# Sparse attention with a gated projection: the products with V in 128x64 instead of 128x32 tiles of TensorE

## The chip, the core and the metric

The kernel runs on one core of a Trainium2 chip. The metric is the device time of one execution in microseconds; lower is better. TensorE works on an array of 128 rows by 128 columns. A matmul whose stationary operand has 32 columns takes a 128x32 part of it (a column tile), one with 64 columns a 128x64 part. In the profile a shape such as 128*32 is rows times columns of the stationary operand, PE are the matmuls and PEld the weight loads that go before them.

## The reference

Eight batches of eight heads, 576 positions, 64 values a head, fp32. Heads 0 to 3 are local (a query sees itself and the 31 positions before it), heads 4 to 7 are strided (a query sees the earlier positions with the same remainder by 32). Then comes a gated projection.

```python
scores = scale * np.matmul(q, k.transpose(0, 1, 3, 2))
mask_local = (rel >= 0) & (rel < 32)
mask_strided = (rel >= 0) & (pos[None, :] % 32 == pos[:, None] % 32)
scores = np.where(masks, scores, -1e9)          # local for h < 4, strided for h >= 4
attn = softmax(scores)                          # exp(s - max) / (sum + 1e-9)
x = np.matmul(attn, v)                          # (B, H, S, 64) -> (B, S, 512)
gate = sigmoid(sum(conv_w[k] * xp[:, k:k + S, :] for k in range(5)))
out = (gate * (x @ w_val)) @ w_out
```

## The kernel before

Everything is planned first and issued later: each step (a matmul group, one vector instruction, one load) gets a number, and the string `SEQUENCE` near the end of the file holds the numbers of all steps in the order of issue, with `f0xN` for N filler matmuls at the start. What one engine executes is its own steps in that order; semaphores are placed from the data and the buffers. TensorE's steps are of these kinds:

- QK, local (`attend_local`, line 301, group `L b.u`): three steps a batch, 12 fp32 matmuls each into `s_ps`, stationary 32 queries (128x32), moving 128 columns.
- QK, strided (`attend_strided`, line 374, group `S b.u`): two steps a batch, 32 fp32 matmuls each into `s_ps`, stationary 128x32, moving 36 columns.
- transposes of the local weights into `t_ps`, 128x128, three or four a step.
- products with V, local: one step for each `L b.u`, 16 fp32 matmuls into `x_ps` (lines 358 to 362). The stationary operand is 32 columns of `vLs`, half a head, the moving one 96 columns of the block-diagonal weights `BDL`. The index `n` counts the four quarters of the 128 output rows, and `n // 2` is the head.
- products with V, strided: two steps for each `S b.u`, 16 matmuls each into `x_ps` (lines 409 to 413), stationary 32 columns of `vSs`, moving 72 columns of `BDS`.
- the value and output projections and, for two chunks of the first batch, the convolution, 128x128 in fp32r into `m_ps`.

There are 24 local and 32 strided steps of products with V in the eight batches. In the order of issue, TensorE goes from a QK step directly to a product with V 18 times (8 of them from local QK, 10 from strided QK), and from a product with V directly to a QK step 19 times (13 to local QK, 6 to strided QK). The other neighbours of these steps are transposes, projections or further products with V. ScalarE copies `x_ps` out, and softmax is shared by VectorE, ScalarE and GpSimd.

`x_ps` has two buffers, `s_ps` two, `t_ps` one, `m_ps` three. All steps are recorded by helpers, so the profile shows one line (L53) for nearly all of them; they are told apart by tile names.

Of the kernel before, what the change touches and what calls it, by code (L numbers as in the profile page):

```python
# [57 lines left out]
def tile_sparse_attention_moe(  # L58
# [34 lines left out]
    def dve(group, fn, **kw):  # L93
        plan.add("dve", group, [(fn, kw)])

    def act(group, fn, **kw):
        plan.add("act", group, [(fn, kw)])

    def gps(group, fn, **kw):
        plan.add("pool", group, [(fn, kw)])  # L100

    def pe(group, calls):
        plan.add("pe", group, calls)

    def mm(out, lhsT, rhs, first=True, last=True):
        return (T.matmul, dict(out=out, lhsT=lhsT, rhs=rhs, start=first, stop=last))
# [17 lines left out]
    vLs = pool.tile([P, 6, 256], F32, name="vLs")  # L124
    vSs = pool.tile([P, 8, 256], F32, name="vSs")
# [175 lines left out]
    def attend_local(b):  # L301
        xs = xss[b % 2]


        for u in range(3):
            group = f"L{b}.{u}"
            sp = s_ps.next()[:, :384]
            sv = sp.rearrange("r (k h w) -> r k h w", h=2, w=64)
            calls = []
            for k, j in enumerate((0, 2, 1)):  # L310
                for a in range(2):
                    for p in range(2):
                        c = 3 * (2 * u + a) + j
                        r0 = 32 * (2 * a + p)
                        calls.append(mm(sv[r0:r0 + 32, k, :, :], qLs[:, p, 32 * c:32 * c + 32],
                                        KBL[:, :, p, 32 * c:32 * c + 64]))
            wide = [P, 3, 2, 64]
            mask, mask_b = (m[:, None, None, :].to_broadcast(wide) for m in (maskL, maskLB))
            if u == 0:
                mask, mask_b = (m[:, :, None, :].to_broadcast(wide) for m in (maskF, maskFB))  # L320
            sm = SML.next()
            recip = softmax(group, sp, calls, mask, mask_b, sm.rearrange("p h k w -> p (h k) w"),
                            sm[..., 0:64].rearrange("p h k w -> p k h w"), "r (k h w) -> r k h w",
                            (b, "L", u) in ONPE).rearrange("p (h k) -> p h k", k=3)
            pw = PB.next()
            packed = pw.rearrange("p h w -> p (h w)")[:, :384]
            ends, middle = pw[:, :, 0:128], pw[:, :, 160:224]
            if b in PACKED:
                ends = packed[:, :256].rearrange("p (h w) -> p h w", h=2)
                middle = packed[:, 256:].rearrange("p (h w) -> p h w", h=2)  # L330
            gps(group, G.tensor_tensor, out=ends.rearrange("p h (k w) -> p h k w", w=64),
                in0=sm[:, :, 0:2, 0:64], in1=recip[:, :, 0:2, None].to_broadcast([P, 2, 2, 64]), op=ALU.mult)
            gps(group, G.tensor_tensor, out=middle, in0=sm[:, :, 2, 0:64],
                in1=recip[:, :, 2:3].to_broadcast([P, 2, 64]), op=ALU.mult)
            bd = BDL.next()
            if b in PACKED:
                tp = t_ps.next()[:, :384].rearrange("r (z g i) -> r z g i", z=3, i=32)
                pe(group, [
                    (T.transpose, dict(out=tp[:, z, :, :].rearrange("r g i -> r (g i)"), in_=packed[:, 128 * z:128 * z + 128],
                                       identity=ident[:, :]))  # L340
                    for z in range(3)])
                act(group, A.copy, out=bd[0:64, :, :, 0, :], in_=tp[0:64, 0:2])
                act(group, A.copy, out=bd[64:128, :, :, 2, :], in_=tp[64:128, 0:2])
                for h in range(2):
                    for i in range(2):
                        act(group, A.copy, out=bd[32 + 32 * i:64 + 32 * i, h, :, 1, :],
                            in_=tp[64 * h + 32 * i:64 * h + 32 * i + 32, 2])
            else:
                tp = t_ps.next().rearrange("r (h z g i) -> r h z g i", h=2, z=2, i=32)
                pe(group, [  # L350
                    (T.transpose, dict(out=tp[:, h, z, :, :].rearrange("r g i -> r (g i)"),
                                       in_=pw[:, h, 128 * z:128 * z + 128], identity=ident[:, :]))
                    for h in range(2) for z in range(2)])
                act(group, A.copy, out=bd[0:64, :, :, 0, :], in_=tp[0:64, :, 0])
                act(group, A.copy, out=bd[64:128, :, :, 2, :], in_=tp[64:128, :, 0])
                act(group, A.copy, out=bd[:, :, :, 1, :], in_=tp[:, :, 1])
            xp = x_ps.next()[:, :384].rearrange("r (p s) -> r p s", p=2)
            pe(group, [
                mm(xp[32 * n:32 * n + 32, p, 96 * a:96 * a + 96],
                   vLs[:, 2 * u + a, 128 * p + 32 * n:128 * p + 32 * n + 32],  # L360
                   bd[:, n // 2, 2 * a + p, :, :].rearrange("r j i -> r (j i)"))
                for a in range(2) for p in range(2) for n in range(4)])
            part = slice(192 * u, 192 * u + 192)
            if b in DIRECT:
                hi, lo = xhi[b % 2][:, 0:2, part], xlo[b % 2][:, 0:2, part]
                act(group, A.copy, out=hi, in_=xp)
                dve(group, V.tensor_tensor, out=lo, in0=xp, in1=hi.bitcast(F32), op=ALU.subtract)
                continue
            act(group, A.copy, out=xs[:, 0:2, PADK:][:, :, part], in_=xp)
        if b not in DIRECT:  # L370
            split_x(b, 0)
            split_x(b, 1)

    def attend_strided(b):
        xs = xss[b % 2]

        n = 16
        for u in range(2):
            group = f"S{b}.{u}"
            sp = s_ps.next()[:, :n * NT]  # L380
            sv = sp.rearrange("r (n t) -> r n t", t=NT)
            calls = []
            for p in range(2):
                for cc in range(4):
                    for g in range(4):
                        r0 = NT * (4 * (4 * u + cc) + g)
                        at = 8 * p + 2 * cc
                        calls.append(mm(sv[32 * g:32 * g + 32, at:at + 2, :],
                                        qSs[:, p * S + r0:p * S + r0 + 32],
                                        KBS[:, :, p, r0:r0 + NT]))  # L390
            pp = PS.next()
            sm = SMS.next()
            wide = [P, n, NT]
            recip = softmax(group, sp, calls, maskS[:, None, :].to_broadcast(wide),
                            maskSB[:, None, :].to_broadcast(wide), sm[:, :, :], sm[:, :, 0:NT],
                            "r (n w) -> r n w", (b, "S", u) in ONPE)

            for rows, keys in ((slice(0, 32, 2), slice(0, 16)), (slice(1, 32, 16), slice(16, NT))):
                gps(group, G.tensor_tensor, out=pp[:, :, rows], in0=sm[:, :, keys],
                    in1=recip[:, :, None].to_broadcast([P, n, keys.stop - keys.start]), op=ALU.mult)  # L400
            pt = PT.next()
            dve(group, V.transpose, out=pt.rearrange("r n t -> r (n t)"), in_=pp.rearrange("r n t -> r (n t)"))
            bd = BDS.next()
            for g in range(4):
                rows = slice(32 * g, 32 * g + 32)
                act(group, A.copy, out=bd[rows, :, g, :], in_=pt[rows, :, 0:NT])
            for p in range(2):
                xp = x_ps.next()[:, :288].rearrange("r (c q) -> r c q", c=4)
                pe(group, [
                    mm(xp[32 * n:32 * n + 32, cc, :],  # L410
                       vSs[:, 4 * u + cc, 128 * p + 32 * n:128 * p + 32 * n + 32],
                       bd[:, 8 * p + 2 * cc + n // 2, :, :])
                    for cc in range(4) for n in range(4)])
                act(group, A.copy,
                    out=xs[:, 2 + p, PADK:].rearrange("r (t c) -> r c t", c=STRIDE)[:, 16 * u:16 * u + 16, :],
                    in_=xp.rearrange("r c (g t) -> r (c g) t", t=NT))
                if u == 1:
                    split_x(b, 2 + p)
# [209 lines left out]
```

## Time and profile before

| what | value |
|---|---|
| median of 3 runs | 311.24 us (309.99 to 311.71) |
| profiled execution, first to last instruction | 308.1 us |
| TensorE busy | 297.6 us (97%) |
| VectorE, ScalarE, GpSimd busy | 75%, 74%, 63% |

The page gives the profiled execution's span, from its first to its last instruction; what lies around it is in the times of the runs alone. A row of the timeline merges instructions of one kind that follow each other: start, length from the first start to the last end, engine, operation, tiles, shapes, count. The start of the last instruction of such a row is start + length - duration of one. An fp32 matmul of the source has two matmul records and two weight loads in the trace. A matmul's end is modelled by the profiler, so the argument goes by starts.

### The profile page before, as it was taken

The page shows a single profiled execution, that of the slowest core. Times are in us where ns is not written, and L with a number is a line of the kernel's source. Part 1 is how long each engine was busy: PE and PEld are TensorE (multiplying, and loading weights), DVE is VectorE, ACT ScalarE, POOL GpSimd, SP SyncE. Part 2 cuts the span into 40 slices and gives each one's busy share as a digit, 9 for nine tenths or more (in the row PEclk, how much of TensorE's full clock was granted, in tenths as well). Part 3 has the DMA queues.
Part 4 walks back from the last instruction along what each step waited for, and adds up shares of the span by engine and source line. Part 5 has one row for each costly group of instructions (what it writes and reads, how often), then busy time and mean ns, then how long its engine had stood idle before and what let it go on. Part 6 is the DMA issues. An engine that isn't in the chain of part 4 may idle for free.

```text
span 308.1 us, 11209 instructions
## 1 busy us (share of the span) xinstructions
PE 297.6 (97%) x4770; PEld 261.4 (85%) x4773; DVE 231.1 (75%) x407; ACT 229.0 (74%) x501; POOL 193.5 (63%) x236
## 2 busy tenths in 40 slices
PE   8697999999999999999999999999999999999995
PEld 3376899988899789998899888998899789989983
DVE  4799499899998859858898788798956786695200
ACT  6667977998689769979989787967987848635221
POOL 8566899968695776558748695666446412562410
PEclk9979999999999999999999999999999999999999
DMA  7999597437655485534635336400133020011003
GB/s 229 351 285 281 191 278 234 139 102 233 207 150 194 145 251 193 158 79 155 190 116 161 96 145 209 141 6 0 70 104 129 36 105 34 3 68 70 0 34 136
DMA packets 20321, 43.99 MB, mean 143 GB/s; under 512 B 3056, under 2 KB 8944, under 8 KB 19696
## 3 DMA queue, kind: packets, MB, share of 16 engines
q1 hardware_dynamic: 20272, 43.28, 43.8%
q8 instruction: 37, 0.61, 0.8%
q14 instruction: 12, 0.10, 0.1%
HBM read 33.84 MB, written 9.44 MB: 140 GB/s over the span
## 4 chain that ended last, share of the span: by engine, by line
PE 89%; DMA 5%; DVE 2%; ACT 1%; POOL 1%; issue 1%; SPq 0%; DVEq 0%; POOLq 0%
PE m_ps L53 66%; PE x_ps L53 11%; PE s_ps L53 8%; PE t_ps L53 4%; DMA xs<-in_w_val_dram 2%; DMA KBL<-in_kL_dram 2%; DMA KBS<-in_kS_dram 1%; DVE ST L53 1%; DVE KBL L173 1%; PE m_ps L162 1%; POOL SML L53 0%; DVE SML L53 0%; POOL PB L53 0%; DVE gate L53 0%; ACT wv L53 0%
## 5 line engine op out<-in xcount | busy, mean ns | idle before, releaser
L53 DVE SCALAR_TENSOR_TENSOR gate<-xs,cw,gate 128x576 f32<-128x576 f32 x120 | 111.6, 948 | 4.8 <-ACT gate L53 4.0
L53 PE MATMUL m_ps<-xhi,wv 128*128 128x288 f32 x512 | 103.7, 297 | 0.0
L53 POOL TENSOR_TENSOR glo<-GV,ghi 128x288 fp32r<-128x288 f32 x64 | 56.0, 883 | 56.1 <-ACT ghi L53 55.7
L53 PE MATMUL m_ps<-wo,ghi 128*128 128x512 f32 x288 | 90.2, 394 | 0.0
L53 PEld LDWEIGHTS m_ps<-xhi,wv 128*128 128x128 f32 x512 | 82.1, 188 | 0.8
L53 PE MATMUL m_ps<-xlo,wv 128*128 128x288 f32 x256 | 75.6, 295 | 0.0
L53 PEld LDWEIGHTS m_ps<-wo,ghi 128*128 128x128 f32 x288 | 52.9, 188 | 11.1 <-issue 0.2
L53 PE MATMUL m_ps<-wo,glo 128*128 128x512 f32 x144 | 56.2, 390 | 0.0
L53 DVE SCALAR_TENSOR_TENSOR GV<-gate,m_ps 128x288 f32<-128x288 f32 x64 | 28.2, 445 | 33.8 <-POOL glo L53 14.2
L53 PEld LDWEIGHTS m_ps<-xlo,wv 128*128 128x128 f32 x256 | 48.1, 188 | 0.0
L53 POOL TENSOR_TENSOR PB<-SML,ST 128x128 f32<-128x128 f32 (+1 forms) x48 | 33.7, 715 | 17.6 <-DVE ST L53 11.6
L53 ACT CAST ghi<-GV 128x288 fp32r<-128x288 f32 x64 | 27.4, 431 | 19.8 <-DVE GV L53 19.2
L53 ACT COPY xs<-x_ps 128x288 f32<-128x288 f32 (+1 forms) x53 | 32.0, 611 | 9.5 <-PE x_ps L53 9.1
L53 ACT COPY BDL<-t_ps 64x256 f32<-64x256 f32 (+2 forms) x108 | 34.3, 319 | 6.2 <-PE t_ps L53 4.5
L53 ACT ACTIVATE osb<-m_ps 128x512 f32<-128x512 f32 x36 | 21.5, 601 | 21.2 <-PE m_ps L53 18.0
L53 PEld LDWEIGHTS m_ps<-wo,glo 128*128 128x128 f32 x144 | 27.0, 188 | 5.9
L53 ACT COPY BDS<-PT 32x288 f32<-32x288 f32 x64 | 27.7, 433 | 2.3 <-PE x_ps L53 1.1
L53 POOL TENSOR_TENSOR xlo<-xs,xhi 128x576 fp32r<-128x576 f32 x16 | 26.5, 1666 | 4.2 <-ACT xhi L53 4.2
L53 POOL TENSOR_TENSOR PS<-SMS,ST 128x256 f32<-128x256 f32 (+1 forms) x32 | 21.0, 669 | 11.7 <-DVE ST L53 11.6
L53 POOL TENSOR_TENSOR SML<-SML,ST 128x384 f32<-128x384 f32 x21 | 23.6, 1129 | 6.0 <-DVE ST L53 6.0
L53 DVE TENSOR_REDUCE ST<-SML 128x6 f32<-128x390 f32 (+1 forms) x45 | 24.2, 543 | 3.0 <-ACT SML L53 2.9
L53 ACT ACTIVATE gate<-xs,cw 128x576 f32<-128x576 f32 x30 | 23.2, 775 | 2.1 <-DVE GV L53 1.9
(91 smaller groups left out, 405.6 us busy)
## 6 DMA issues: line engine op xcount, KB each, us to landing
out_dram<-osb SPq DMA_DIRECT2D x36, 256.0 KB, 2.3
vLs<-in_vL_dram SPq DMA_DIRECT2D x8, 640.0 KB, 6.4
qLs<-in_qL_dram SPq DMA_DIRECT2D x16, 288.0 KB, 4.2
KBL<-in_kL_dram SPq DMA_DIRECT2D x16, 288.0 KB, 4.6
KBS<-in_kS_dram SPq DMA_DIRECT2D x16, 288.0 KB, 5.0
qSs<-in_qS_dram SPq DMA_DIRECT2D x16, 288.0 KB, 3.6
vSs<-in_vS_dram SPq DMA_DIRECT2D x32, 128.0 KB, 5.1
raw<-in_w_val_dram SPq DMA_DIRECT2D x2, 512.0 KB, 6.4
```

The costliest lines, as they stand in the source:

```text
L53: fn(**kw)
L162: plan.filler = lambda at: T.matmul(out=at, lhsT=idle[:, :P], rhs=idle[:, :], start=True, stop=True)
L173: [(lambda out: eng.memset(out, value), dict(out=ap))])
```

## The change

The four matmuls with 32 columns of V (`n` from 0 to 3) become two with 64 (`h` from 0 to 1): each multiplies a head's 64 columns at once. The moving operand, the output rows and columns, the order of steps, `SEQUENCE`, the buffers and the copies are as they were. QK keeps its 32 columns, since 32 queries make up its stationary operand.

```diff
             pe(group, [
-                mm(xp[32 * n:32 * n + 32, p, 96 * a:96 * a + 96],
-                   vLs[:, 2 * u + a, 128 * p + 32 * n:128 * p + 32 * n + 32],
-                   bd[:, n // 2, 2 * a + p, :, :].rearrange("r j i -> r (j i)"))
-                for a in range(2) for p in range(2) for n in range(4)])
+                mm(xp[64 * h:64 * h + 64, p, 96 * a:96 * a + 96],
+                   vLs[:, 2 * u + a, 128 * p + 64 * h:128 * p + 64 * h + 64],
+                   bd[:, h, 2 * a + p, :, :].rearrange("r j i -> r (j i)"))
+                for a in range(2) for p in range(2) for h in range(2)])
...
                 pe(group, [
-                    mm(xp[32 * n:32 * n + 32, cc, :],
-                       vSs[:, 4 * u + cc, 128 * p + 32 * n:128 * p + 32 * n + 32],
-                       bd[:, 8 * p + 2 * cc + n // 2, :, :])
-                    for cc in range(4) for n in range(4)])
+                    mm(xp[64 * h:64 * h + 64, cc, :],
+                       vSs[:, 4 * u + cc, 128 * p + 64 * h:128 * p + 64 * h + 64],
+                       bd[:, 8 * p + 2 * cc + h, :, :])
+                    for cc in range(4) for h in range(2)])
```

## Rows read from the trace of the kernel before

**Rows 1.** The page: parts 1 and 4, busy time and the chain that ended last.
```profile
span 308.1 us, 11209 instructions
PE 297.6 (97%) x4770; PEld 261.4 (85%) x4773; DVE 231.1 (75%) x407; ACT 229.0 (74%) x501; POOL 193.5 (63%) x236
...
PE 89%; DMA 5%; DVE 2%; ACT 1%; POOL 1%; issue 1%; SPq 0%; DVEq 0%; POOLq 0%
```

**Rows 2.** Two stretches: length, busy us (instructions) by engine, granted clock, DMA share, GB/s.
```profile
0.00:41.00 41.00, 34.66 (x725) 25.12 (x728) 29.77 (x62) 29.95 (x63) 29.82 (x55) 0.96 0.83 266
41.00:308.00 267.00, 262.96 (x4045) 236.31 (x4045) 201.34 (x346) 199.00 (x438) 163.72 (x182) 1.00 0.39 124
```

**Rows 3.** Instructions by tile: min/median/max ns of one, first and last start us, form.
```profile
L53 PEld LDWEIGHTS x_ps<-BDS,vSs x1024: 106/110/110, 30.8 to 265.1; 128*32 128x32 f32 x171
L53 PE MATMUL x_ps<-BDS,vSs x1024: 222/226/251, 30.8 to 265.2; 128*32 128x72 f32 x171
...
L53 PE MATMUL x_ps<-BDL,vLs x768: 242/246/271, 20.3 to 243.2; 128*32 128x96 f32 x192
...
L53 PE MATMUL s_ps<-KBS,qSs x1024: 193/197/269, 16.4 to 207.3; 128*32 128x36 f32 x171
...
L53 PE MATMUL s_ps<-KBL,qLs x576: 269/273/297, 9.0 to 196.9; 128*32 128x128 f32 x192
...
L53 PE MATMUL t_ps<-ident,PB x84: 270/273/476, 14.5 to 236.9; 128*128 128x128 f32 x84
...
L53 PE MATMUL m_ps<-xhi,wv x512: 288/294/403, 41.3 to 290.4; 128*128 128x288 f32 x171
```

**Rows 4.** Timeline of PE, 60.6 to 68 us: start us, length us, what.
```profile
60.62 1.21 PE L53 MATMUL x_ps<-BDS,vSs 128*32 128x72 f32 x64
61.65 0.84 PE L53 MATMUL s_ps<-KBL,qLs 128*32 128x128 f32 x24
...
66.64 1.18 PE L53 MATMUL x_ps<-BDS,vSs 128*32 128x72 f32 x64
67.75 0.66 PE L53 MATMUL t_ps<-ident,PB 128*128 128x128 f32 x4
```

**Rows 5.** Timeline of PE, 46.7 to 50.8 us.
```profile
46.70 0.86 PE L53 MATMUL s_ps<-KBL,qLs 128*32 128x128 f32 x24
47.38 0.84 PE L53 MATMUL x_ps<-BDL,vLs 128*32 128x96 f32 x32
...
49.36 0.84 PE L53 MATMUL s_ps<-KBL,qLs 128*32 128x128 f32 x24
50.13 0.66 PE L53 MATMUL t_ps<-ident,PB 128*128 128x128 f32 x4
```

**Rows 6.** Timeline of PE, 114.3 to 115.5 us.
```profile
114.32 0.49 PE L53 MATMUL t_ps<-ident,PB 128*128 128x128 f32 x3
114.74 0.71 PE L53 MATMUL x_ps<-BDS,vSs 128*32 128x72 f32 x32
```

**Rows 7.** Timeline of PE at three waits (idle before, and what ended it).
```profile
24.21 0.87 PE L53 MATMUL x_ps<-BDL,vLs 128*32 128x96 f32 x32 [0.35 <-DVE xlo L53]
...
37.34 0.76 PE L53 MATMUL s_ps<-KBS,qSs 128*32 128x36 f32 x64 [0.23 <-DMA KBS<-in_kS_dram]
...
90.76 0.77 PE L53 MATMUL s_ps<-KBS,qSs 128*32 128x36 f32 x64
91.59 1.21 PE L53 MATMUL x_ps<-BDS,vSs 128*32 128x72 f32 x64
```

**Rows 8.** Timeline of PE at 140 and 158 us.
```profile
140.05 1.22 PE L53 MATMUL s_ps<-KBL,qLs 128*32 128x128 f32 x24
141.16 1.21 PE L53 MATMUL x_ps<-BDS,vSs 128*32 128x72 f32 x64
...
157.98 1.49 PE L53 MATMUL s_ps<-KBL,qLs 128*32 128x128 f32 x48
159.31 0.29 PE L53 MATMUL x_ps<-BDL,vLs 128*32 128x96 f32 x4
```

## The prediction

> **What bounds the kernel now.** I read the page first: TensorE is busy in 297.6 of 308.1 us, and 89% of the chain that ended last is its own work [rows 1]. Then the busy time by stretches: up to 41 us TensorE is busy in 34.66 of 41.00 us, from there on in 262.96 of 267.00 us at a granted clock of 1.00, which is the upper of its two levels [rows 2]. So from 41 us to the end every nanosecond added to TensorE's stream should appear in the time, and one taken away should shorten it; before that, DMAs and other engines end some waits and there is slack.
>
> A busy share does not tell how full the engine is, so next come the single instructions [rows 3] and a stretch of the timeline [rows 4]. Each fp32 matmul of the source has two records, each with its own weight load. A strided group pair has 64 matmul records: it lasts 1.21 us, the last record of it 0.226 us, so from the first start to the last it is 0.98 us [rows 3, 4]. Four column tiles take part, 16 records each. I call four records that run beside each other a round: 15 rounds lie between the first and the last, less some 0.02 us by which the fourth tile starts after the first, and less 0.025 us of the first weight load (a group's first matmul lasts 251 ns, the others 226). That makes (0.98 - 0.045) / 15 = 0.0625 us a round for 72 columns. The local products between two others of their width have 32 records in 0.84 us [rows 5]: (0.84 - 0.246 - 0.02) / 7 = 0.082 us a round for 96 columns; QK with 24 records: (0.84 - 0.273 - 0.02) / 5 = 0.109 us for 128. So a round costs 0.83 ns a column and some 2.5 ns on top. It is bound by the columns that stream, not by the number of instructions. The transposes give the cross-check: one 128x128 tile, 128 columns, three records, (0.49 - 0.273) / 2 = 0.109 us each [rows 6]. One tile of 128 columns of the array and one of 32 stream at the same pace, so I take it that one of 64 does too.
>
> **The change part by part.**
>
> *Removed: half of the matmuls.* 24 local groups go from 16 to 8 matmuls, 32 strided ones from 16 to 8: 448 fewer, 896 records with as many loads. Each round is now two records side by side, not four, and the number of rounds stays: a group had 16 x 2 / 4 = 8 rounds, and has 8 x 2 / 2 = 8. At the same pace this is worth 0, except that the second tile, not the fourth, is the last to start: (20 - 7) ns = 13 ns earlier at the end of a run of such groups.
>
> *Added: wider weight loads.* The extra time of a first matmul, which can't hide its load, is 251 - 226 = 25 ns for 32 columns and 403 - 294 = 109 ns for 128 [rows 3]. On the line between them 64 columns need 53 ns. Inside a group it hides beside the tile's previous matmul, 62.5 or 82 ns long: nothing, with 9 ns to spare in the strided groups. Without that cover, at the far end of 109 ns a load, 256 strided rounds would take 47 ns more and 192 local ones 27 ns more, 17 us; at the near end of 25 ns nothing. I take 53, since both ends of the line are of the same kind, fp32 words over 128 rows, and 64 lies on the near side. At the start of a run, where it doesn't hide, it costs 53 - 25 = 28 ns.
>
> *Added: boundaries between two widths.* This carries the sum. QK stays at 32 columns; the products with V go to 64. In the written order a product with V directly follows QK 18 times, and QK directly follows such a product 19 times. Today both have 128x32 tiles and run into each other: after the last strided product starts (60.62 + 1.21 - 0.226 = 61.60) QK starts at 61.65, 0.045 us later [rows 4]; after the last QK matmul (46.70 + 0.86 - 0.274 = 47.286) the local product starts at 47.38, 0.09 us later [rows 5]. Where the width changes it takes longer: from the last strided product at 66.64 + 1.18 - 0.226 = 67.594 to the transpose at 67.75 it is 0.156 us [rows 4], from the last QK at 49.36 + 0.84 - 0.273 = 49.927 to the transpose at 50.13 it is 0.203 us [rows 5], and the other way, from a transpose's last at 114.32 + 0.49 - 0.273 = 114.537 to a product at 114.74, 0.203 us [rows 6]. Less the streaming of the last matmul (62.5 or 109 ns) each leaves 94 ns in which nothing starts: the array empties first. Against the boundary without a change of width the first matmul behind it starts 0.203 - 0.09 = 0.113 us later.
>
> No row shows a change between 32 and 64 columns. It is bounded by 0 (the array takes the other width without emptying) and by these 113 ns. I take 113, since the empty time is the same 94 ns out of 32 columns and out of 128, so it hangs on the change and not on the widths, and every 64-column tile overlaps two 32-column ones that are at work. [...]
>
> Price of entering from QK: 113 + 53 (the first load is no longer fetched ahead, as behind every change of width) = 166 ns. Of leaving to QK: 113 - 13 + 25 = 125 ns. Of the 18 entries one lies before 41 us behind a wait for VectorE (24.21), and two later ones wait for ScalarE longer than 0.203 us, as the one at 91.59, 0.26 us behind QK [rows 7]: 3 are free. Two more start late already and pay only a part [rows 8]: at 141.16, 0.16 us behind the last QK matmul (140.05 + 1.22 - 0.273 = 141.00), 203 - 160 + 53 = 96 ns, and at 159.31, 0.11 us behind (157.98 + 1.49 - 0.273 = 159.20), 203 - 110 + 53 = 146 ns. 13 pay in full: 2.16 + 0.24 = 2.40 us. Of the 19 exits three lie before 41 us, ahead of waits for DMA and VectorE (the last is QK at 37.34) [rows 7]: 16 x 0.125 = 2.00 us. Runs that begin behind a transpose or a 128-wide product change width already: 15 after 41 us pay 28 ns, 0.42 us. Runs that end in such a change gain 13 ns, 16 of them, -0.21 us.
>
> Sum: 2.40 + 2.00 + 0.42 - 0.21 = +4.6 us on a span of 308.1. The median of the runs is 311.24, 3.1 us above that span; what lies around it is not touched. Predicted: 311.2 + 4.6 = 315.8 us.
>
> **Who else could become late.** ScalarE, VectorE and GpSimd get their inputs some 0.1 us later at each boundary and have their own slack; TensorE's later groups find operands readier than now. No wait is added, no buffer changes hands, and the DMAs are untouched.
>
> **The rivals.**
>
> *No emptying between 32 and 64 columns.* Then only the longer first loads at width changes that exist today remain, 0.42 - 0.21 us: 311.4. [...] Against: 94 ns at every change of width that is shown. 12%.
>
> *Faster, by relief of the instruction stream.* A strided QK group of 64 records lasts 0.77 us at 90.76 [rows 7], 0.57 from first to last start, while 15 rounds of 36 columns at the pace above are 15 x 32.5 + 20 = 0.51 us. So 16 such groups lose 0.06 us each, 1.0 us, as if instructions came too slowly; with half of the records ahead of them gone, and with no emptying, the time would be 311.4 - 1.0 = 310.4, and with half of the chain's issue time (1% of 308.1 us [rows 1]) gone too 308.9. It decides only if too few instructions are ready when such a group starts; but the one at 37.34, which stood behind a wait of 0.23 us while its instructions could come up, lasts 0.76 us as well, and the one at 90.76 follows a slow projection [rows 7]. 5%.
>
> *Slower by far: loads of 64 columns don't hide, or two wide tiles don't run beside each other.* From 62.5 ns a load on it lengthens each strided round. With 53 ns fully open in 448 rounds it is 24 us more, about 335; with two tiles one after the other, 256 x 62.5 + 192 x 82 ns, 32 us more, about 343. Against it: loads of 32 columns hide fully today in rounds of 62.5 ns. [...] 5% for open loads, 4% for tiles one after the other.
>
> **How the numbers follow.** The forecast has 74%. A measurement of this kernel can tell about 0.5% (1.6 us) from no change. Faster: 0.06. Same: the case without emptying and the tail of the forecast, 0.13. Slower: 0.81. Range: down to 311.2, which takes in the case without emptying; up, with first loads at the 109 ns of 128 columns (15 x 56 ns at entries and 15 at present changes, 1.7 us, 317.5) and one more us for strided rounds lengthened by 4 ns, 318.6. Left out are the gain and most of the far slower case.
>
> **What would show it.** Right: products with V in 128x64 records, 384 and 512, that last as long as now; a group as long as now less some 13 ns; loads of 64 columns near 110 + 28 = 138 ns [rows 3]; 0.2 us between the last QK matmul and the first local product at 47.4 us, and a first product longer by about 53 ns; the added time spread over some 29 boundaries, none of it inside the groups. Wrong: boundaries that stay at 0.045 and 0.09 us; rounds longer than 62.5 or 82 ns; strided QK groups that get shorter.

## The result and the profile after

The changed kernel took 314.82 us (median of 4 runs, 313.69 to 315.46), the kernel before 310.62 us beside it: 1.42% slower, with a 95% interval of 0.96% to 1.89%. The forecast was 315.8 us, 1.5% over the median then known.

The page of the changed kernel, parts 1 and 4 and one line of part 3 (kind of DMA queue: packets, MB, share), to be set beside [rows 1]:

```profile
span 313.5 us, 9417 instructions
PE 301.9 (96%) x3874; PEld 262.7 (84%) x3877; DVE 231.1 (74%) x407; ACT 228.9 (73%) x501; POOL 192.8 (61%) x236
...
q8 instruction: 30, 0.49, 0.7%
...
PE 87%; DMA 7%; DVE 2%; ACT 1%; issue 1%; POOL 0%; SPq 0%; DVEq 0%; POOLq 0%
```

896 matmul records are gone, as forecast, and TensorE is busy for 4.3 us longer. The single instructions, to be set beside [rows 3], in the same columns:

```profile
L53 PEld LDWEIGHTS x_ps<-BDS,vSs x512: 132/137/137, 30.6 to 270.5; 128*64 128x64 f32 x171
L53 PE MATMUL x_ps<-BDS,vSs x512: 225/226/278, 30.7 to 270.6; 128*64 128x72 f32 x171
...
L53 PE MATMUL x_ps<-BDL,vLs x384: 246/246/297, 19.3 to 248.7; 128*64 128x96 f32 x192
```

A product lasts what it did, 226 and 246 ns. A load of 64 columns has 137 ns (138 was forecast), and the first product of a group is 52 or 51 ns longer than the others (53 was forecast). Now the stretches of [rows 4] and [rows 5] in the timeline of the changed kernel (start, length, what):

```profile
62.50 1.22 PE L53 MATMUL x_ps<-BDS,vSs 128*64 128x72 f32 x32
63.65 0.86 PE L53 MATMUL s_ps<-KBL,qLs 128*32 128x128 f32 x24
...
68.81 1.22 PE L53 MATMUL x_ps<-BDS,vSs 128*64 128x72 f32 x32
69.96 0.66 PE L53 MATMUL t_ps<-ident,PB 128*128 128x128 f32 x4
```

The strided pair with half of the records takes 1.22 us, as long as before. From its last start, 62.50 + 1.22 - 0.226 = 63.494, to QK it is 0.156 us, where it was 0.045; and from there to the transpose, 68.81 + 1.22 - 0.226 = 69.804 to 69.96, it is 0.156 us, as it was [rows 4]. So a change from 64 to 32 columns costs the same as one from 32 to 128.

This profiled execution is 5.4 us longer than that of before, more than the medians differ. The waits of TensorE tell why (engine and tile, what ended the wait: us in total, times, longest):

```profile
PE x_ps L53 <- DMA vLs<-in_vL_dram: 1.3, 2, 1.0
...
PE s_ps L53 <- DVE GV L53: 0.4, 1, 0.4
```

Twice it waited for a load of V, for 1.0 us at 48.97 and for 0.3 us at 76.39, and once for VectorE, for 0.4 us at 46.62. Of the other three executions of the changed kernel one has a span of 313.5 us too, and two have 311.8 and 312.2 us. The clearest pair to compare is the kernel before and the changed kernel with a shift of its code (an experiment below), whose trace has none of these waits. In it the local stretch that corresponds to [rows 5] reads:

```profile
45.43 0.86 PE L57 MATMUL s_ps<-KBL,qLs 128*32 128x128 f32 x24
46.23 0.88 PE L57 MATMUL x_ps<-BDL,vLs 128*64 128x96 f32 x16
47.04 0.86 PE L57 MATMUL s_ps<-KBL,qLs 128*32 128x128 f32 x24
47.83 0.88 PE L57 MATMUL x_ps<-BDL,vLs 128*64 128x96 f32 x16
48.64 0.86 PE L57 MATMUL s_ps<-KBL,qLs 128*32 128x128 f32 x24
49.43 0.66 PE L57 MATMUL t_ps<-ident,PB 128*128 128x128 f32 x4
```

From the first QK group to the transpose it is 4.00 us, before it was 50.13 - 46.70 = 3.43 [rows 5]: two entries and two exits cost 0.57 us, where the forecast's prices make 2 x (166 + 125) = 582 ns. This stretch also shows the way from 32 to 64 columns: from the last QK matmul at 47.04 + 0.86 - 0.273 = 47.627 to the product at 47.83 it is 0.203 us, as forecast, where it was 0.09 [rows 5].

### The profile page after: what moved, and what is told of

Its sections match the earlier page's. It is cut to its first block, busy times and chain, and to the rows that moved or that the text cites. A ratio compares the mean times of both kernels' runs of the same rounds, so it can differ in the third digit from the quotient of the medians.

```text
span 313.5 us, 9417 instructions
## 1 busy us (share of the span) xinstructions
PE 301.9 (96%) x3874; PEld 262.7 (84%) x3877; DVE 231.1 (74%) x407; ACT 228.9 (73%) x501; POOL 192.8 (61%) x236
## 4 chain that ended last, share of the span: by engine, by line
PE 87%; DMA 7%; DVE 2%; ACT 1%; issue 1%; POOL 0%; SPq 0%; DVEq 0%; POOLq 0%
PE m_ps L53 62%; PE x_ps L53 11%; PE s_ps L53 8%; DMA vLs<-in_vL_dram 5%; PE t_ps L53 3%; PE m_ps L162 3%; DMA xs<-in_w_val_dram 2%; DVE gate L53 1%; DVE ST L53 1%; ACT xs L53 1%; ACT xhi L53 0%; DVE SML L53 0%; POOL PB L53 0%; ACT gate L53 0%; SPq L53 0%
```

## The experiments

Each time is compared with the kernel before on the same chip.

**Half of the change.** First only the local products are wide, then only the strided ones.

Only the local ones wide (the strided lines stay as they were):

```diff
-                mm(xp[32 * n:32 * n + 32, p, 96 * a:96 * a + 96],
-                   vLs[:, 2 * u + a, 128 * p + 32 * n:128 * p + 32 * n + 32],
-                   bd[:, n // 2, 2 * a + p, :, :].rearrange("r j i -> r (j i)"))
-                for a in range(2) for p in range(2) for n in range(4)])
+                mm(xp[64 * h:64 * h + 64, p, 96 * a:96 * a + 96],
+                   vLs[:, 2 * u + a, 128 * p + 64 * h:128 * p + 64 * h + 64],
+                   bd[:, h, 2 * a + p, :, :].rearrange("r j i -> r (j i)"))
+                for a in range(2) for p in range(2) for h in range(2)])
```

> Only the local products with V in 128x64 tiles, the strided ones in 128x32 as before. Boundaries theory: behind 41 us 11 entries from 32 to 64 columns (one of them starts late anyway) and 12 exits from 64 to 32, some of them now between local and strided products; at 166 and 125 ns, with +28 ns at 7 runs that begin behind a 128-wide step and -13 ns at 6 that end in one, +3.4 us over before, about 314. Rival, the wide tiles themselves are slower (loads that do not hide): 192 of 448 rounds are wide, so under half of the 4.2 us, +1.8. Rival, the later transfers that after's profile shows near 47 to 49 and 76 us (2.1 us of waits): about +2, with no growth at the boundaries.

Measured: 313.83 us, 1.18% (0.84 to 1.53) over before.

Only the strided ones wide (the local lines stay as they were):

```diff
-                    mm(xp[32 * n:32 * n + 32, cc, :],
-                       vSs[:, 4 * u + cc, 128 * p + 32 * n:128 * p + 32 * n + 32],
-                       bd[:, 8 * p + 2 * cc + n // 2, :, :])
-                    for cc in range(4) for n in range(4)])
+                    mm(xp[64 * h:64 * h + 64, cc, :],
+                       vSs[:, 4 * u + cc, 128 * p + 64 * h:128 * p + 64 * h + 64],
+                       bd[:, 8 * p + 2 * cc + h, :, :])
+                    for cc in range(4) for h in range(2)])
```

> Only the strided products with V in 128x64 tiles, the local ones in 128x32. Boundaries theory: behind 41 us 6 full entries, one in part and two free ones that wait for ScalarE anyway, 7 exits, 8 runs that begin and 10 that end at a 128-wide step: +2.1 us, about 313; together with the local-only kernel more than the whole change (5.5 against 4.6), since local and strided products then change width among themselves. Rival, wide tiles slower in themselves: 256 of 448 rounds, the tighter ones, over half of 4.2 us: +2.4 or more, and less than the whole change together with the local-only kernel. Rival, late transfers: about +2 wherever they fall.

Measured: 313.63 us, 1.32% (0.91 to 1.74) over before, some 4.1 us where 2.1 was expected. Together the halves cost more than the whole, as the boundaries would have it, but by too much. Both traces have a kind of wait that is next to absent in the kernel before (0.4 us in all). First the timeline with only the local products wide, then two lines of the waits with only the strided ones wide:

```profile
118.38 0.68 PE L53 MATMUL x_ps<-BDS,vSs 128*32 128x72 f32 x32
121.06 0.53 PE L53 MATMUL m_ps<-xhi,wv 128*128 128x288 f32 x2 [2.00 <-issue]
```

```profile
PE m_ps L53 <- issue: 2.7, 1, 2.7
...
PE x_ps L53 <- issue: 1.4, 1, 1.4
```

TensorE stood for 2.0 us, and for 2.7 and 1.4 us, for nothing that the profile shows but its own sequencer. Less these, and with the 0.36 us that the kernel before stands in the same way, the stretch from the first value projection behind 40 us to the last output projection is longer than before by 4.50 - 2.00 + 0.36 = 2.9 us (3.4 expected) and by 6.17 - 4.1 + 0.36 = 2.4 us (2.1 expected). So the sums fit to half a microsecond. The single boundaries are clearer. With only the local products wide, the time from the start of a local product to that of the strided QK behind it grows by 126 to 152 ns at its four places behind 41 us, and from a strided product to the local QK behind it by 0 or 1 ns at its five; with only the strided ones wide it is 0 ns and 99 to 129 ns.

**Wide tiles away from QK.** 64 columns only in the 13 steps whose run of products has no QK step beside it.

```diff
+    def wide_v(step):
+        return 64 if step in APART else 32
...
+                mm(xp[w * n:w * n + w, p, 96 * a:96 * a + 96],
+                   vLs[:, 2 * u + a, 128 * p + w * n:128 * p + w * n + w],
+                   bd[:, n * w // 64, 2 * a + p, :, :].rearrange("r j i -> r (j i)"))
+                for w in [wide_v((b, "L", u))] for a in range(2) for p in range(2) for n in range(128 // w)])
```

`APART` lists the 13 steps (L0.0, L7.0 to L7.2, one of S0.1, both of S2.1, S6.1, S7.0 and S7.1); the strided lines are written in the same way.

> 128x64 only in the runs of products with V that have no QK step on either side: 13 of 56 steps. No boundary between 32 and 64 columns is made. Boundaries theory: +28 ns at 5 runs and -13 ns at 5, +0.1 us, the same as before within the measurement; the rounds of these groups stay at 62.5 and 82.5 ns. Rival, wide tiles slower in themselves: 13 of 56 of 4.2 us, +1.0 us, with longer rounds in the trace of these groups.

Measured: 318.82 us, 2.78% (2.36 to 3.2) over before. Neither theory has room for this: no boundary was added, and the 13 steps did not get slower. The time lies in five stretches without instructions; the waits, and the longest one in the timeline:

```profile
PE x_ps L53 <- issue: 5.2, 3, 3.1
...
PE m_ps L53 <- issue: 2.6, 2, 2.1
```

```profile
47.97 0.83 PE L53 MATMUL x_ps<-BDL,vLs 128*32 128x96 f32 x29
51.85 0.37 PE L53 MATMUL x_ps<-BDL,vLs 128*32 128x96 f32 x2 [3.05 <-issue]
51.86 0.52 PE L53 MATMUL s_ps<-KBL,qLs 128*32 128x128 f32 x3
```

It stopped in the middle of a group, 29 records of 32 in, and the group is a narrow one. The DMA view of the ten microseconds up to there (kind of queue: packets, MB, share of the engines' time), first of this kernel, then of before in the like stretch:

```profile
q1 hardware_dynamic: 1333, 2.94, 95.1%
```

```profile
q1 hardware_dynamic: 1316, 2.86, 93.4%
q8 instruction: 2, 0.03, 1.6%
```

Before loads two blocks of code in this time, at 45.64 and 49.42 us. In this kernel the loads on either side start at 38.46 and at 49.56 us; the second takes 1.10 us, no longer than others (0.88 to 1.36 us in before), but it starts 0.8 us after TensorE has stopped. The theory that follows: TensorE's code comes in blocks of 16 KB, 37 in before by the line below and 30 in the changed kernel, whose pages have 4770 + 4773 and 3874 + 3877 records of TensorE, 37.3 and 30.3 times 256, so 256 to a block; and where the edge of a block falls in the stream decides whether a load is late.

```profile
q8 instruction: 37, 0.61, 0.8%
```

**The code shifted.** More TensorE instructions at the start, where it waits for the first loads anyway: long fillers (512 columns) are replaced by more short ones (64 columns). This moves the edges of the blocks by 64, 128 or 192 of 256 instructions; the steps behind 10 us and their order stay.

For 128 instructions, in `SEQUENCE` and where the tokens are read (for 64 it is `f0x14 g36`, for 192 `f0x5 g109`; a filler has two instructions):

```diff
-f0x18
+f0x9 g73
...
+            if token.startswith("g"):
+                for _ in range(int(token[1:])):
+                    self.small()
+                continue
...
+    plan.small = lambda: T.matmul(out=plan.spare[0][:, :64], lhsT=idle[:, :P], rhs=idle[:, :64], start=True, stop=True)
```

> The kernel with 128x64 only away from QK, and 64 more TensorE instructions at the start (4 long filler matmuls replaced by 36 short ones, which take about the same time in the wait for the first loads). Its 8 us over before came as five stretches in which TensorE had no work and waited for nothing but its sequencer (3.2 us at 48.6, 2.2 at 122, 1.1 at 148, 1.4 at 181, 0.5 at 218), each with a 16 KB code load on the instruction queue that came late. Code-loading theory: the load falls at every 256th instruction, and 64 more put the code between 37 and 98 us where it lies in before: the stall at 48.6 goes, the others move; at most 5 us over before, at best 0.1. Rival, wide tiles slower in themselves: nothing changes, 318.8.

Measured: 310.21 us, ratio 0.9998 (0.9971 to 1.0026): the 8 us are gone, with the same 13 wide steps; behind 41 us TensorE waits for its sequencer for 0.24 us. A strided pair among them, the wide one of this kernel and the narrow one of before:

```profile
96.87 1.22 PE L57 MATMUL x_ps<-BDS,vSs 128*64 128x72 f32 x32
```

```profile
97.81 1.21 PE L53 MATMUL x_ps<-BDS,vSs 128*32 128x72 f32 x64
```

So wide tiles in themselves cost nothing, and code that comes late cost 8 us. The control has no wide tile at all:

> The kernel before with 192 more TensorE instructions at the start (13 long filler matmuls replaced by 109 short ones), which is 64 fewer as the 256-instruction blocks of the code loads count: from 37 us on the same place as in the kernel with 128x64 away from QK, without a wide tile in it. Code-loading theory: a stall of about 3 us near 48 us without any wide tile, perhaps others, 312 to 318. Rival, wide tiles slower in themselves: same as before, 310.

Measured: 313.44 us, 1.23% (0.72 to 1.73) over before. Its trace has one wait for the sequencer, 1.8 us at 50 us, where 3 us at 48 was expected, and 0.9 us for a load of V. The wait stands in the same group at the same record as the longest one with wide tiles away from QK:

```profile
49.21 0.83 PE L57 MATMUL x_ps<-BDL,vLs 128*32 128x96 f32 x29
51.87 0.27 PE L57 MATMUL x_ps<-BDL,vLs 128*32 128x96 f32 x2 [1.83 <-issue]
```

> The kernel before with 128 more TensorE instructions at the start (9 long filler matmuls replaced by 73 short ones). Code-loading theory: its stalls fall elsewhere; how many can't be told, 0 to 8 us over before. Rival: same as before.

Measured: 317.85 us, 2.67% (2.07 to 3.28) over before, with not one instruction of the work changed. Its waits:

```profile
PE m_ps L57 <- issue: 5.8, 5, 2.5
...
PE x_ps L57 <- issue: 2.4, 3, 1.5
```

> The kernel before with 64 more TensorE instructions at the start. With the shifts of 0, 128 and 192 this makes the four quarters of a 256-instruction code block. Code-loading theory: somewhere from 0 to 8 us over before, and all of it, within half a microsecond, in stretches of the trace in which TensorE waits for its sequencer. Rival, the short fillers themselves cost: more with more of them, none in single stretches.

Measured: 312.79 us, 0.68% (0.37 to 0.99) over before. Its waits for the sequencer are 2.1 us, but a wait of 1.5 us for a load of V comes with them; so, against the expectation, not all that TensorE loses lies in waits for the sequencer. The rival of this run is out: the time does not grow with the number of short fillers (0.68%, 2.67% and 1.23% for 36, 73 and 109 of them).

> The changed kernel with the same 128 instructions more at the start. Boundaries theory: 0.2 us between the last QK matmul and the next product with V, and 0.16 to 0.18 us the other way, at every one of the places as before, whatever the stalls of code loading do; these may add 0 to 8 us or nothing to 314.8.

Measured: 313.19 us, 1.16% (0.76 to 1.57) over before. TensorE waits for its sequencer nowhere behind 41 us. This is the trace that was read above. Its stretch from the first value projection behind 39 us to the last output projection, against the same of before:

```profile
39.93 0.40 PE L57 MATMUL m_ps<-xhi,wv 128*128 128x288 f32 x1
...
293.28 0.40 PE L57 MATMUL m_ps<-wo,ghi 128*128 128x512 f32 x1
```

```profile
41.30 0.40 PE L53 MATMUL m_ps<-xhi,wv 128*128 128x288 f32 x1
...
290.62 0.40 PE L53 MATMUL m_ps<-wo,ghi 128*128 128x512 f32 x1
```

253.35 us against 249.32: 4.0 us more. By the starts of all groups in the two traces, 1.6 us of it lie between a QK group and the product behind it (17 places), 2.1 us between a product and the QK group behind it (16 places), 0.1 us behind QK groups whose first load is open now, 0.2 us behind runs of products that end at another step, and no more than 0.1 us anywhere else. The kernel before stands 0.36 us at 140.8 us without instructions and this one does not, so the boundaries cost 4.4 us. The list of TensorE's matmul waits lacks this one, since the modelled ends of the matmuls cover it; the weight loads show it (their timeline in before):

```profile
140.79 0.22 PEld L53 LDWEIGHTS s_ps<-KBL,qLs 128*32 128x32 f32 x8 [0.36 <-issue]
```

In four kernels that have no boundary at this place (only the local products wide, and before with its code shifted by 64, 128 and 192) the time from this QK group to the product behind it is 0.45 us shorter than in before; by that the boundaries cost 4.5 us.

The expectation of 0.2 us from the last QK matmul to the next product holds behind local QK (202 to 203 ns), not behind strided QK, where it is 125 or 126 ns. The other way it is 176 ns from a local product and 155 or 156 ns from a strided one, as expected. Less the streaming of the last matmul (109, 82 and 62.5 ns, and 32.5 for strided QK by the forecast's price of a column) all four leave 93 to 94 ns.

> The changed kernel with 64 more TensorE instructions at the start. Boundaries theory: less its stretches without instructions it stands 4 to 4.5 us over the kernel before without its own, about 313 to 314; with them up to 8 us more. Rival, the 1.4% are luck of the code loads: at some shift it is as fast as before at its best, 309 to 310.

Measured: 315.43 us, 1.52% (1.05 to 2.0) over before, with 1.2 us of waits for the sequencer.

> The changed kernel with 192 more TensorE instructions at the start. As for the shift of 64: not under 313 if the boundaries cost what the trace shows, 309 to 310 if luck of the code loads made the difference.

Measured: 314.89 us, 1.31% (0.61 to 2.02) over before, with 1.0 us of such waits.

The prices of the boundaries are the same to 2 ns in the traces of the changed kernel at all four shifts, at every place but the two entries that wait for ScalarE and one entry at a shift of 0 (148 ns for 126). In the kernel before, the time from a strided product to local QK, for example, is 42 to 44 ns at every shift (14 or 15 at one of the five places).

All eight, as a ratio to the kernel before at a shift of 0 (the waits are sums of the rounded rows of the profile, over the whole trace):

| instructions more | before | waits for the sequencer, us | changed | waits for the sequencer, us |
|---|---|---|---|---|
| 0 | 1 | 0.4 | 1.0142 | 0.2 |
| 64 | 1.0068 | 2.1 | 1.0152 | 1.2 |
| 128 | 1.0267 | 8.4 | 1.0116 | 0 |
| 192 | 1.0123 | 1.8 | 1.0131 | 1.0 |

At no shift is the changed kernel under 1.0116, and the boundaries' 4.4 us stay at every shift: they are not luck. Which of the two kernels is faster is another matter. The kernel before stands at the best of its four places, and the mean of the four is 1.0115, against 1.0135 for the changed one; at 128 the changed kernel is the faster. In these traces late code costs the changed kernel less (0 to 1.2 us, against 0.4 to 8.4 us); that it has some 1800 instructions fewer may be the reason, but no run shows that. None of these kernels beats the one before at a shift of 0.

What ends these waits can be read from the single loads. All 13 traces together have 21 waits for the sequencer of 0.4 us or more behind 24 us. In each the load of a 16 KB block ends 1.2 to 1.6 us before TensorE goes on, and each stands at the same place of the stream: counted from the start, 193 or 194 records of TensorE (matmuls, weight loads and its sequencer's) behind a multiple of 256. I read this as TensorE standing at the edge of a block until the next block is there.

**The price of one change of width.** The strided products of the changed kernel alternate between 64 and 32 columns.

```diff
-                    for cc in range(4) for h in range(2)])
+                    for cc in range(4) for w in [(64, 32)[cc % 2]] for n in range(128 // w)])
```

> The changed kernel with its strided groups at 64, 32, 64, 32 columns for the four chunks: three more changes of width inside each of 32 strided steps, one more between 12 neighbouring pairs, 8 exits to QK fewer; rounds, columns and results as they were. Boundaries theory: 64 to 32 costs 94 + 7 + 25 = 126 ns, 32 to 64 costs 94 + 20 + 53 = 167 ns, so 419 ns a step, of which some 29 lie behind 41 us: +12.2 + 1.8 - 1.0 = +13 us over the changed kernel, about 328. Rival, no emptying between the two widths, only first loads that do not hide: 25 + 53 + 25 ns a step, +3.9 us, about 318. Rival, late transfers: no more than the changed kernel.

Measured: 328.05 us, 5.9% (5.48 to 6.32) over before; 328 was expected, 318 without emptying. The strided pair of [rows 4], which takes 1.22 us in the changed kernel:

```profile
68.39 0.86 PE L53 MATMUL s_ps<-KBL,qLs 128*32 128x128 f32 x24
69.18 2.22 PE L53 MATMUL x_ps<-BDS,vSs 128*64 128x72 f32 x48
71.34 0.66 PE L53 MATMUL t_ps<-ident,PB 128*128 128x128 f32 x4
```

Seven changes inside the pair (four down, three up) cost 1.00 us; the expected prices make 4 x 126 + 3 x 167 = 1005 ns.

## Why the prediction was right, step by step

- *TensorE bounds the kernel from 41 us on.* Right: of 4.6 us forecast, 4.4 arrived there. The two levels of the granted clock in the trace of before are 0.50 (from 16 to 19 us) and 1.00 (all the way from 41 to 308 us).
- *Rounds are bound by columns; half the matmuls are worth nothing.* Right: 32 records take the time of 64 (1.22 us a strided pair for 1.21), in the changed kernel and in the shifted kernel with the wide tiles away from QK, whose ratio is 0.9998.
- *A load of 64 columns needs 53 ns and hides inside a group.* Right: 51 to 52 ns at the first product of a group, nothing inside, where the others last 226 and 246 ns as before.
- *The array empties between 32 and 64 columns.* This was the open step, between 0 and 113 ns. 0.156 us from the last strided product to QK, with 62.5 ns of streaming in it, leaves the forecast 94 ns, and 0.203 us from the last local QK matmul to the product, with 109 ns in it, leaves 94 ns as well; the sum of the seven changes in a pair of the alternating kernel fits that price. The rival without emptying is out: between 32 and 64 columns, too, there are 94 ns in which nothing starts. What the runs show is this pause of 93 to 94 ns at the changes of width that were read; that the array empties in it is the author's reading, and no run shows it.
- *The count of boundaries.* 4.4 us of the 4.6 forecast, or 4.5 with the 0.45 us at 140 us; where the rest went was not followed place by place. Ten of the 18 entries come from strided QK, of which the forecast had read no boundary without a wait; the 94 ns are the same there. One reading was wrong: the 0.16 us at 141.16 [rows 8] were taken as this place's own, but a wait for the sequencer lies in the QK group before it, and it is gone when the code is shifted.
- *No wait is added.* Not so in every trace. Waits for a load of V, of which the kernel before has none, stand in the changed kernel at shifts of 0 (1.3 us) and 192 (0.3 us), and also in the kernel before at shifts of 64 (1.5 us), 128 (0.2 us) and 192 (0.9 us). So they do not need a wide tile; what sets them off was not followed.
- *Relief of the instruction stream.* The forecast gave this 5% and placed it in the strided QK groups. They stayed as they were; one in the changed kernel has 64 records in 0.77 us, as at 90.76 before [rows 7]:

```profile
58.80 0.77 PE L53 MATMUL s_ps<-KBS,qSs 128*32 128x36 f32 x64
59.51 0.88 PE L53 MATMUL x_ps<-BDL,vLs 128*64 128x96 f32 x16
```

  What instructions can cost lies in another place: it is the late code, which the kernel before happens to miss. The pause that the forecast priced is there, 94 ns at a boundary, and that its number came out was in part luck, since both kernels stand at places with little late code; a shift of 128 instructions would have made the kernel before the slower one by 1.5%. No step of the forecast had this term, and what it cost here (0 to 8.4 us) is wider than the range given.
- *The range.* It took in the case without emptying at its lower end, which the runs exclude.

## What to carry to other kernels

Here a wider tile in place of two narrow ones that already run side by side gave nothing (1.22 us a strided pair for 1.21); count instead how often neighbours in the order have tiles of different widths, and price each at the empty time that the timeline shows at such a change (here 94 ns, with the first load open behind it: 25 ns for 32 columns, 51 to 52 for 64). Before a difference of 1 or 2% between two kernels with different numbers of instructions is put down to the work, look in the list of waits for stretches in which the engine waits for its own sequencer, and shift the code with a few fillers to see what remains (here such stretches were 0 to 8.4 us, and the boundaries' 4.4 us remained).

## What the runs showed of the hardware that was not expected

TensorE stood for up to 3.05 us at a time behind code loads that came late. Its instructions come on a queue of their own (37 loads before and 30 in the changed kernel on q8, while the other instruction queue, q14, has 12 in both), in blocks of 0.61 MB / 37 = 16 KB; the changed kernel has 896 matmul records and as many weight loads less, 7 x 256 in all, and 7 blocks less. Shifts of the same stream by 64, 128 and 192 instructions lengthened the time by 0.7, 2.7 and 1.2% (2.1, 8.3 and 3.8 us), and the traces have 2.1, 8.4 and 1.8 us of waits for the sequencer (the longest 2.5 us, and 3.05 us in the kernel with wide tiles away from QK). The late loads are not slow, they start late: the three behind the longest waits (3.05, 2.73 and 2.50 us) took 1.0 to 1.2 us (0.88 to 1.36 us in before) and started only after TensorE had stopped. In the clearest case no load started for 11 us, while the data queue took 95% of the DMA engines' time (93% in the like stretch of before, which loaded two blocks); but a stretch of 2.5 us at 121 us in the shifted kernel before followed a run of narrow products as well, so whether busy DMA engines or the dense instructions make a load late was not tried and stays open.
